# Padding zeros written on chip, 64-row query loads, and a planner order shifted by a table of moves

## Chip, cores and metric

One Trainium2 chip, one core. The metric is the device time of one execution in microseconds (us). The kernel before takes 840.61 us, the median of 3 runs (840.38 to 841.45).

## What is computed

Block-causal attention over 4 batches of 8 heads (576 positions, 64 dimensions), then two feed-forward layers on the 2304 tokens. The reference, cut to what matters:

```python
scores = scale * np.matmul(q, k.transpose(0, 1, 3, 2))
mask = block_i >= block_j                      # blocks of 64 positions
scores = np.where(mask, scores, -1000000000.0)
scores = scores - np.max(scores, axis=-1, keepdims=True)
attn = np.exp(scores)
attn = attn / (np.sum(attn, axis=-1, keepdims=True) + 1e-09)
attn_out = np.matmul(attn, v)                  # then to x, 2304 tokens by 512
h = np.maximum(np.maximum(x @ w1, x @ w2), x @ w3)      # 512 -> 768
x = h @ w_out                                           # 768 -> 512
h = np.maximum(x @ w_in, 0.0)                           # 512 -> 2048
return h * h @ w_out                                    # 2048 -> 512
```

## The kernel before, in words

The program has two parts. The **first part** (`fused_kernel` down to the first `nc.issue()`, line 862) holds all attention, the first feed-forward layer of four of the six token blocks (`mlp1(0)` to `mlp1(3)`) and the preparation of the weights. The **second part** holds `mlp1(4)`, `mlp1(5)` and the second feed-forward layer (`up`, `down`: tiles `ph_x`, `ph_z`, `acc_x`, `acc_z`, `acc_y`).

Attention goes by pairs of heads: 16 pairs, 4 per batch. A pair's `step(i)` makes, for 128 queries and two heads, the scores (`sc` in PSUM), writes the mask value into a corner and takes the row maximum on VectorE (`nm`), takes the exponential on ScalarE (`P`, with the row sums `sm`), transposes `P` on TensorE (`tp`) and copies the result back to SBUF (`ta`, `tb`); `values` multiplies with V (`av`). A pair has 25 transposes. The first four pairs (batch 0) are split in two groups of queries: group 0 (256 queries, steps 0 and 1) of all four pairs runs first, so that block 0 of the feed-forward layer can start.

Scores of two heads that share a tile are kept apart by zeros: head 0's queries stand in partitions 0 to 63 of one tile (`z[0]`), head 1's in partitions 64 to 127 of another (`z[1]`), and the other 64 partitions of each are zero. In `score_operands_f32` (line 499) these zeros come with the transfer: the input array `z0` holds them, and a 128x256 transfer (128 KB) brings each half of group 0. The tiles are `zk` (pairs 0 and 1) and `zk_early` (pairs 2 and 3), with the keys in the third slot.

The first feed-forward layer (`mlp1_`, tiles `l`, `run`, `hh`, `hl`, `ys`) is TensorE's filler: 288 matmuls for each block, whose blocks are 256, 320, 432, 432, 432 and 432 tokens wide. Its weights come as raw 64-bit numbers (`raw_w`, `raw_wo`, 512 KB each, 24 chunks) and are turned into a high and a low part (`w1h`, `w1l`, `wo`) by a chain for each chunk: two ScalarE passes, two VectorE passes, one GpSimd addition, one ScalarE cast, one VectorE subtraction (`load_w_`, line 398).

The order is set by a planner (`Plan`). The code only notes operations; `issue` (line 229) then plays them with fixed costs, picks at each step the engine that could start first, and on it the operation of lowest rank, then lowest number:

```python
t = min(start.values())
i = min((i for i, s in start.items() if s <= t), key=lambda i: (ops[i].rank, i))
```

Each engine runs its instructions in the order in which they were issued. All transfers go through SyncE's one queue; the built program keeps eight of their semaphores in turn, so that a transfer is issued only when the one eight before it has landed.

Of the kernel before, what the change touches and what calls it, by code (L numbers as in the profile page):

```python
# [12 lines left out]
F32 = mybir.dt.float32  # L13
# [10 lines left out]
B, H, S, D = 4, 8, 576, 64  # L24
# [13 lines left out]
TAIL = 512  # L38

GROUPS = ((0, 256), (256, 320))  # L40
GA, GB = 256, 320
# [6 lines left out]
CFG = dict(PD=-1, PE=1, A1=0, A2=0, WP=1, FC=(8, 16), WO=24, FI=0, LO2=0, HI2=0, Q2=0, RN=3, XL=2, HL=2, SO=0, TF=0, W_A=0.7, W_B=1.5, SPARE='hl..rhl..rhl..r..r..r', S=15, PB=3, QB=(2, 2, 3), BANKS=(3, 2, 1, 2), LO=0, HI=0, Q=0, EV=('*', '*'), EV2=('a', 'a'), CB=2, PC=0, PM=1000, PX=-0.5, PO=0, HH='*', XH='*', N0='a', YS='a', HIS=0, RB=1, TB=(1, 1), KB=1, CT='a', LT='d', XA=4, XB=0)  # L48
# [44 lines left out]
class View:  # L93


    def __init__(self, tile, area, steps=()):
        self.tile, self.area, self.steps = tile, area, steps
# [50 lines left out]
        return View(t, t.area)  # L148


class Op:
    def __init__(self, index, engines, name, args, kw, rank):
        self.index, self.engines, self.name, self.args, self.kw, self.rank = index, engines, name, args, kw, rank
        self.deps, self.after, self.makes = set(), [], []
        self.engine = self.end = None

# [15 lines left out]
class Plan:  # L172
# [53 lines left out]
            (v.tile.writes if any(v is x for x in out) else v.tile.reads).append((op, v.area))  # L226
        return op

    def issue(self):

        ops, free, held, queue = self.ops, self.free, self.held, self.queue
        left = [0 for op in ops]
        users = [[] for _ in ops]
        for op in ops:
            for d in (*op.deps, *op.after):
                if d.end is None:
                    left[op.index] += 1
                    users[d.index].append(op)
        waiting = {e: {} for e in free}
        narrow = False  # L240

        def offer(op):
            for e in op.engines:
                when = 0.0
                for d in op.deps:
                    when = max(when, d.end + ((SEM[d.engine] + (500 if e == 'pe' else 100 if e == 'pool' else 0)) if d.engine != e else 0))
                waiting[e][op.index] = when, shares_port(e, op)

        for op in ops:
            if not left[op.index]:  # L250
                offer(op)
        for _ in ops:
            best = None
            for e, w in waiting.items():
                if not w:
                    continue
                other = held["pool" if e == "dve" else "dve"] if e in held else 0.0
                start = {i: max(free[e], at, other if port else 0.0) for i, (at, port) in w.items()}
                t = min(start.values())
                i = min((i for i, s in start.items() if s <= t), key=lambda i: (ops[i].rank, i))  # L260
                if best is None or t < best[0]:
                    best = t, e, i
            t, e, i = best
            op = ops[i]
            op.engine = e
            length = duration(e, op) * SLOW[e]
            if e == "pe":
                length += SWITCH * (columns(op) != narrow)
                narrow = columns(op)
            if e in held and waiting[e][i][1]:  # L270
                held[e] = t + length - HOLD[e]
            for other in op.engines:
                del waiting[other][i]
            if e == "sp":
                queue = max(t + 1700, queue) + transfer(op)
                op.end, free[e] = queue + 300, t + 465
            else:
                op.end = t + length
                free[e] = op.end - LAP[e]
            for tile in op.makes:  # L280
                tile.make()
            self.tc.keep_in_program_order(self.call(self.real[e], alias(e, op.name), op.args, op.kw))
            for u in users[i]:
                left[u.index] -= 1
                if not left[u.index]:
                    offer(u)
        self.ops, self.queue = [], queue
# [15 lines left out]
def width(x):  # L303
    return math.prod(x.area.shape[1:])
# [5 lines left out]
def columns(op):  # L310
    return op.name != "transpose" and width(op.args[1] if op.args[1:] else op.kw["lhsT"]) <= 64


def alias(engine, name):
    return {"act": "copy", "dve": "tensor_copy"}.get(engine, name) if name in ("copy", "tensor_copy") else name


def shares_port(engine, op):
    if engine not in ("dve", "pool"):
        return False  # L320
    sources = [x for k, x in op.kw.items() if k.startswith("in") and isinstance(x, View) and not x.psum]
    if engine == "pool" or len(sources) > 1:
        return bool(sources)
    return bool(sources) and not op.kw["out"].psum and width(op.kw["out"]) % 2 == 0 and op.name != "tensor_reduce"


def duration(engine, op):
    views = op.views()
    n = max(map(width, views))
    psum = any(x.psum for x in views)  # L330
    if engine == "pe":
        if op.name == "transpose":
            return 109
        stat = op.args[1] if op.args[1:] else op.kw["lhsT"]
        n = width(op.args[0])
        if stat.tile.args[1] == F32:
            return n * (0.842 if width(stat) <= 64 else 1.69)
        return 1 + 0.4527 * n
    if engine == "act":
        if op.name == "activation":  # L340
            return 340 + 0.87 * n if "accum_out" in op.kw else 195 + 0.95 * n
        return 157 + 0.84 * n if psum else 190 + 0.85 * n
    if engine == "pool":
        return 160 + 2.26 * n
    if engine == "sp":
        return 430
    if op.name == "memset":
        return 58 + 0.84 * n
    if op.name == "reciprocal":
        return 160  # L350
    if op.name in ("tensor_scalar", "tensor_copy", "copy") and not psum:
        return (210 if isinstance(op.kw.get("scalar1"), View) else 155) + 0.52 * n
    return 150 + 1.046 * n


def transfer(op):
    x = next(v for v in op.views())
    return 35 + x.area.shape[0] * 4 * width(x) / 385.0
# [3 lines left out]
def fused_kernel(ctx: ExitStack, tc: tile.TileContext, z0, k0, kz0, qk, v, w123, wo1, win2, wo2, out):  # L362
    nc = Plan(tc)
# [19 lines left out]
    at = Pool(nc, es_a.enter_context(tc.tile_pool(name="at", bufs=1, side="right", reuse_waits="tile")))  # L383
# [115 lines left out]
    def score_operands_f32(n, g):  # L499


        if g == 0:
            if n < 2:
                zk = at.tile([128, 3, GA], F32, tag="tb", bufs=2 * CFG["TB"][1], name=f"zk{n}")
            else:
                if not early:
                    early.append(m1.tile([128, 8, 3, GA], F32, tag="wo1", name="zk_early"))
                zk = early[0][:, n]
            z, k = [zk[:, h] for h in range(2)], zk[:, 2]
            parts = (0, GA), (GA, GA)  # L510
        else:
            parts = (2 * GA, TAIL - GA + 128), (TAIL + GA + 128, TAIL - GA)
            z = [at.tile([128, w], F32, tag=t, bufs=CFG["QB"][2 * (t == "kl")], name=f"z{n}_{t}")
                 for t, (_, w) in zip(("qs", "kl"), parts)]
            k = at.tile([128, S], F32, tag="kh", bufs=CFG["QB"][1], name=f"k{n}")
        (o0, w0), (o1, w1) = parts
        nc.sync.dma_start(out=z[0], in_=z0[n, :, o0:o0 + w0])
        nc.sync.dma_start(out=k, in_=k0[n, :, :GROUPS[g][0] + GROUPS[g][1]])
        nc.sync.dma_start(out=z[1], in_=z0[n, :, o1:o1 + w1])
        return [[(z[h], k)] for h in range(2)], [(z[0][:, TAIL - GA:], k)] if g else None  # L520

    def value_operands(n, g):
        chunks = 2 if n < NPAIR and g == 0 else 5
# [4 lines left out]
    ops, x_t = {}, {}  # L528
# [16 lines left out]
    def prefetch(n, g):  # L545


        f32 = bool(n < NPAIR and g == 0 or S_F32[n])
        with nc.ranked(CFG["PO"]):
            ops[n] = f32, score_operands_f32(n, g) if f32 else score_operands(n), value_operands(n, g)  # L550
# [306 lines left out]
    with nc.behind(marks[CFG["WO"]][0]), nc.ranked(2):  # L857
        for q in range(NQ):
            quad_forms(1, q)
        for q in range(EARLY):  # L860
            quad_forms(0, q)
    nc.issue()
    es_a.close()


# [310 lines left out]
```

## Time and profile before

| | |
|---|---|
| median of 3 runs | 840.61 us |
| profiled execution, its own time | 840.18 us |
| its span, first to last instruction | 838.4 us |
| TensorE (PE) busy in the span | 825.8 us, 99% |
| VectorE (DVE) busy | 625.0 us, 75% |
| ScalarE (ACT) busy | 474.4 us, 57% |
| GpSimd (POOL) busy | 108.0 us, 13% |
| HBM read / written | 150.47 MB / 38.80 MB |

Shares over the whole span hide that the two parts differ: the first part ends near 364 us, and from there on TensorE runs one matmul after the other to the end. A busy TensorE is not one at its peak, since the ends of matmuls are modelled and overlap; what one matmul costs in a full stream is read from long unbroken pieces of the chain.

### The profile page before, as it was taken

The numbers are of one execution on the slowest core, as the hardware profiler recorded it, in microseconds if no ns is written. First come the engines' busy times: TensorE is split into PE (matmuls) and PEld (weight loads), VectorE is DVE, ScalarE is ACT, GpSimd is POOL, SyncE is SP. The second block draws the span as 40 slices with busy tenths as digits, with TensorE's granted clock in tenths as the row PEclk, the third lists the DMA queues.
The fourth block names the chain that finished last, engine by engine and source line by source line (L and its number), as shares of the span: only waits on it lengthen the run. The fifth ranks groups of instructions, "written<-read, shape, count | busy, mean of one in ns | idle before, by whom it ended". The sixth has DMA issues, their size and how long they took to land.

```text
span 838.4 us, 14621 instructions
## 1 busy us (share of the span) xinstructions
PE 825.8 (99%) x5008; PEld 779.2 (93%) x5008; DVE 625.0 (75%) x1347; ACT 474.4 (57%) x1099; POOL 108.0 (13%) x98
## 2 busy tenths in 40 slices
PE   8999999999999999999999999999999999999998
PEld 6678899988999889999999999999999999999998
DVE  7989789888889988817877557987269855478562
ACT  7999678788778767736554224544124552233441
POOL 2343111221122212202221000000000000000000
PEclk9999999999999999999999999999999999999999
DMA  9755455665566656254796867888988889988882
GB/s 326 263 162 171 124 175 182 203 224 183 167 206 206 199 192 201 77 194 150 264 352 228 312 203 248 286 292 271 306 257 255 257 249 288 293 256 254 246 272 85
DMA packets 92203, 190.24 MB, mean 227 GB/s; under 512 B 9697, under 2 KB 18913, under 8 KB 92129
## 3 DMA queue, kind: packets, MB, share of 16 engines
q1 hardware_dynamic: 92128, 189.31, 69.2%
q8 instruction: 40, 0.66, 0.3%
q14 instruction: 35, 0.28, 0.1%
HBM read 150.47 MB, written 38.80 MB: 226 GB/s over the span
## 4 chain that ended last, share of the span: by engine, by line
PE 90%; DVE 5%; ACT 3%; DMA 1%; POOL 1%; issue 1%; POOLq 0%; ACTq 0%; DVEq 0%
PE l L190 33%; PE ph_x L190 12%; PE acc_x L190 12%; PE ph_z L190 9%; PE acc_z L190 6%; PE av L190 4%; PE sc L190 4%; PE tp L190 3%; PE acc_y L190 3%; PE sc_t L190 2%; DVE nm L190 1%; DMA raw_w<-in_wo 1%; PE tp_t L190 1%; DVE w1l L190 1%; ACT P L190 1%
## 5 line engine op out<-in xcount | busy, mean ns | idle before, releaser
L190 PE MATMUL l<-xhl,w1h 128*128 128x432 f32 (+2 forms) x864 | 230.6, 344 | 0.5 <-DVE xhl L190 0.5
L190 PEld LDWEIGHTS l<-xhl,w1h 128*128 128x128 f32 x864 | 154.0, 188 | 7.5 <-DVE xhl L190 1.2
L190 PE MATMUL l<-xhl,w1l 128*128 128x432 f32 (+2 forms) x432 | 149.7, 347 | 0.6 <-DVE run L190 0.5
L190 PEld LDWEIGHTS l<-xhl,w1l 128*128 128x128 f32 x432 | 81.3, 188 | 5.8 <-DVE run L190 1.4
L190 PE MATMUL ph_x<-t,ws 128*128 128x384 f32 x432 | 80.9, 335 | 0.0
L190 PE MATMUL l<-hh,wo 128*128 128x432 f32 (+2 forms) x288 | 77.5, 344 | 1.2 <-DVE wo L190 1.1
L190 PEld LDWEIGHTS ph_x<-t,ws 128*128 128x128 f32 x432 | 75.6, 188 | 0.0
L190 ACT ACTIVATE P<-sc,nm 128x128 f32<-128x128 f32 (+3 forms) x128 | 67.3, 535 | 11.5 <-DVE nm L190 10.0
L190 DVE TENSOR_TENSOR run<-l,run 128x432 f32<-128x432 f32 (+2 forms) x72 | 39.8, 553 | 32.6 <-PE l L190 29.4
L190 POOL TENSOR_TENSOR f_w<-f_w,raw_w 128x512 int32<-128x512 int32 x30 | 41.5, 1384 | 148.2 <-DVE f_w L190 33.4
L190 DVE TENSOR_REDUCE nm<-sc 128x2 f32<-128x256 f32 (+2 forms) x96 | 55.0, 590 | 0.8
L190 PEld LDWEIGHTS l<-hh,wo 128*128 128x128 f32 x288 | 51.9, 188 | 3.7 <-DVE wo L190 1.3
L190 PE MATMUL acc_x<-g_p,ws 128*128 128x384 f32 x288 | 54.0, 335 | 0.0
L190 PE MATMUL ph_z<-b,ws 128*128 128x384 f32 x288 | 53.9, 335 | 0.0
L190 PE MATMUL tp<-ident,P 128*128 128x128 f32 x320 | 49.9, 275 | 1.1 <-ACT rs L190 0.5
L190 PEld LDWEIGHTS acc_x<-g_p,ws 128*128 128x128 f32 x288 | 50.5, 188 | 0.0
L190 PEld LDWEIGHTS ph_z<-b,ws 128*128 128x128 f32 x288 | 50.4, 188 | 0.0
L190 PE MATMUL l<-hl,wo 128*128 128x432 f32 (+2 forms) x144 | 49.2, 342 | 0.0
L190 PEld LDWEIGHTS tp<-ident,P 128*128 128x128 f32 x320 | 38.8, 141 | 8.9 <-ACT P L190 1.3
L190 PE MATMUL av<-tb,v 128*64 128x320 f32 (+1 forms) x256 | 42.9, 410 | 0.0
L190 ACT COPY tb<-tp 128x384 f32<-128x384 f32 (+1 forms) x64 | 32.4, 539 | 13.4 <-PE tp L190 12.9
L190 DVE TENSOR_TENSOR g_p<-c_wo,g_p 128x768 fp32r<-128x768 f32 x24 | 22.9, 956 | 16.8 <-ACT g_p L190 16.8
(188 smaller groups left out, 1746.5 us busy)
## 6 DMA issues: line engine op xcount, KB each, us to landing
ws<-ws_d SPq DMA_DIRECT2D x336, 256.0 KB, 4.0
ws_d<-wst SPq DMA_DIRECT2D x70, 256.0 KB, 4.4
raw<-in_qk SPq DMA_DIRECT2D x24, 576.0 KB, 4.3
ws_d<-wst SPq DMA_DIRECT2D x21, 512.0 KB, 7.1
raw_w<-in_w SPq DMA_DIRECT2D x18, 512.0 KB, 4.8
raw_w<-in_wo SPq DMA_DIRECT2D x16, 512.0 KB, 4.3
raw_wi<-in_win SPq DMA_DIRECT2D x14, 512.0 KB, 5.8
v<-in_v SPq DMA_DIRECT2D x16, 320.0 KB, 3.8
```

Of the source, the lines that this page charges most:

```text
L190: return getattr(engine, op_name)(*map(value, args), **{k: value(x) for k, x in kw.items()})
```

## The change

In group 0 of pairs 0 to 3, GpSimd writes the zeros (two memsets of 64x256 for each pair, rank -2), and the transfers bring the 64 filled partitions alone. The other case of `score_operands_f32` is written out again without a difference. `issue` takes a table of moves: for some 430 operations of the first part it adds a number to the rank and another to the place that decides between equal ranks. The planner also gets a cost for a GpSimd memset.

```diff
+MOVES = (
+    (8, -18, 7349), (18, -21.5, -8878), (19, -16.5, -4442), (20, -16, -3840), (21, -15.5, 1495), (43, -12.5,
...
+)
...
+        self.place = rank, index
...
-    def issue(self):
+    def issue(self, moves=()):
...
+        for i, rank, place in moves:
+            ops[i].place = ops[i].rank + rank, ops[i].index + place
...
-                i = min((i for i, s in start.items() if s <= t), key=lambda i: (ops[i].rank, i))
+                i = min((i for i, s in start.items() if s <= t), key=lambda i: ops[i].place)
...
+    if engine == "pool" and op.name == "memset":
+        return 100 + 0.8 * n
...
-            parts = (0, GA), (GA, GA)
...
+            with nc.ranked(-2):
+                nc.gpsimd.memset(z[0][64:128], 0.0)
+                nc.gpsimd.memset(z[1][0:64], 0.0)
+            nc.sync.dma_start(out=z[0][0:64], in_=z0[n, 0:64, 0:GA])
+            nc.sync.dma_start(out=k, in_=k0[n, :, :GA])
+            nc.sync.dma_start(out=z[1][64:128], in_=z0[n, 64:128, GA:2 * GA])
+            return [[(z[h], k)] for h in range(2)], None
...
-    nc.issue()
+    nc.issue(MOVES)
```

The same instructions are issued as before, and eight memsets; three copies that either ScalarE or VectorE may do go to VectorE instead of ScalarE. The order changes on every engine. Three places:

**SyncE, the first transfers.** `raw_w_0_0`, `raw_w_0_1` and `raw_w_0_2` are the first weight chunks, `zk` the queries (from `in_z`) and keys (from `in_k`) of pairs 0 and 1, `zk_early` those of pair 2, `v` the values. Before:

```order
L190 DMA raw_w_0_0_80<-in_w 128x1024
L190 DMA zk_82<-in_z 128x256
L190 DMA zk_82<-in_k 128x256
L190 DMA zk_82<-in_z 128x256
L190 DMA v_0_93<-in_v 128x256
L190 DMA raw_w_0_1_97<-in_w 128x1024
L190 DMA zk_99<-in_z 128x256
L190 DMA zk_99<-in_k 128x256
L190 DMA zk_99<-in_z 128x256
L190 DMA v_0_103<-in_v 128x256
L190 DMA raw_w_0_2_105<-in_w 128x1024
L190 DMA zk_early<-in_z 128x256
```

Now:

```order
L256 DMA raw_w_0_0_80<-in_w 128x1024
L256 DMA v_0_82<-in_v 128x256
L256 DMA zk_84<-in_z 64x256
L256 DMA zk_84<-in_k 128x256
L256 DMA zk_84<-in_z 64x256
L256 DMA raw_w_0_1_106<-in_w 128x1024
L256 DMA zk_91<-in_z 64x256 x2
L256 DMA zk_91<-in_k 128x256
L256 DMA v_0_112<-in_v 128x256
L256 DMA raw_w_0_2_114<-in_w 128x1024
L256 DMA zk_early<-in_z 64x256
L256 DMA zk_early<-in_k 128x256
```

The values of pair 0 moved ahead of its queries, and the five query loads here carry 64 partitions instead of 128.

**ScalarE, from the first weight chunk to the first exponentials** (`P_0_0`, `P_1_0`: steps 0 and 1 of pair 0). Before:

```order
L190 ACTIVATE raw_w_0_0_80<-raw_w_0_0_80 128x512 x2
L190 ACTIVATE raw_w_0_1_97<-raw_w_0_1_97 128x512
L190 CAST w1h_136<-raw_w_0_0_80 128x512
L190 ACTIVATE P_0_0_145,sm_0_146<-sc_0_0_117,nm_0_128 128x128 x2
L190 ACTIVATE P_1_0_158,sm_0_146<-sc_1_0_119,nm_1_133 128x256 x2
```

Now:

```order
L256 ACTIVATE raw_w_0_0_80<-raw_w_0_0_80 128x512 x2
L256 ACTIVATE raw_w_0_1_106<-raw_w_0_1_106 128x512 x2
L256 CAST w1h_149<-raw_w_0_0_80 128x512
L256 ACTIVATE P_0_0_160,sm_0_161<-sc_0_0_125,nm_0_134 128x128 x2
L256 ACTIVATE P_1_0_171,sm_0_161<-sc_1_0_129,nm_1_140 128x256 x2
```

The second pass over chunk `raw_w_0_1` moved ahead of the first exponentials.

**TensorE, the first scores and transposes** (pairs 0, 1 and 2). Before:

```order
L190 MATMUL sc_0_0_117<-zk_82 128x128
L190 MATMUL sc_1_0_119<-zk_82 128x256
L190 MATMUL sc_0_0_117<-zk_82 128x128
L190 MATMUL sc_1_0_119<-zk_82 128x256
L190 MATMUL sc_0_0_149<-zk_99 128x128
```

Now:

```order
L256 MATMUL sc_0_0_125<-zk_84 128x128 x2
L256 MATMUL sc_1_0_129<-zk_84 128x256 x2
L256 MATMUL sc_0_0_151<-zk_91 128x128 x2
L256 MATMUL sc_1_0_158<-zk_91 128x256 x2
L256 MATMUL tp_0_0_173<-ident,P_0_0_160 128x128 x2
```

Both heads of step 0 now stand before step 1, where the heads were taken one after the other.

## Rows read from the trace of the kernel before

**Rows 1.** The page's section 1, whole execution.

```profile
PE 825.8 (99%) x5008; PEld 779.2 (93%) x5008; DVE 625.0 (75%) x1347; ACT 474.4 (57%) x1099; POOL 108.0 (13%) x98
```

**Rows 2.** Windows: busy us and count of PE, PEld, DVE, ACT, POOL; clock; DMA.

```profile
0.00:100.00 100.00, 92.30 (x668) 73.08 (x669) 84.54 (x216) 84.93 (x217) 34.24 (x30) 1.00 0.63 211
100.00:364.00 264.00, 262.74 (x1710) 240.59 (x1709) 227.63 (x652) 201.09 (x565) 54.51 (x54) 1.00 0.57 184
...
372.00:485.00 113.00, 113.00 (x580) 108.45 (x579) 79.47 (x140) 53.96 (x99) 19.27 (x14) 1.00 0.70 248
...
10.00:20.00 10.00, 8.99 (x67) 6.04 (x66) 9.95 (x31) 9.59 (x32) 3.87 (x3) 1.00 1.02 369
```

**Rows 3.** Chain of waits in order of time: start us, us, what.

```profile
46.52 3.94 PE l L190 x33
...
157.33 1.31 PE l L190 x9
...
304.11 0.48 PE sc_t L190 x2
...
308.20 0.17 PE sc L190 x2
308.81 0.24 PE sc L190 x2
309.44 0.35 PE sc L190 x2
310.56 0.87 PE tp L190 x8
...
321.69 0.93 PE sc L190 x4
...
338.35 3.01 PE av L190 x23
...
364.29 120.32 PE l L190 x614
...
826.46 8.35 PE acc_x L190 x48
```

**Rows 4.** Groups of PE by form, to 364.2 us: xcount | busy us, mean ns | idle.

```profile
L190 PE MATMUL r<-ident,sm 128*64 128x128 f32 x64 | 5.0, 277 | 0.9 <-DVE nm L190 0.6 <-DVE sm L190 0.2
```

**Rows 5.** Waits of PE, longest first: us in total, times, longest us.

```profile
PE sc L190 <- DMA zk<-in_k: 1.4, 1, 1.4
...
PE l L190 <- DVE wo L190: 1.1, 1, 1.1
...
PE sc_t L190 <- ACT P L190: 0.5, 1, 0.5
```

**Rows 6.** Timeline, first 14 us: start us, us, engine, instruction, [idle before <-releaser].

```profile
0.73 0.20 POOL masks.py:197 MEMSET ident<- 128x128 f32 x1 [0.29 <-POOLq L1169]
...
1.36 3.78 PE L190 MATMUL idle<-ident 128*128 128x128 f32 x16 [1.36 <-POOL ident masks.py:199]
...
4.40 1.24 ACT L190 ACTIVATE raw_w<-raw_w 128x512 f32<-128x512 f32 x2 [2.18 <-DMA raw_w<-in_w]
5.10 0.43 DVE L190 TENSOR_SCALAR raw_w<-raw_w 128x512 int32<-128x512 int32 x1 [4.24 <-ACT raw_w L190]
...
5.27 2.04 PE L190 MATMUL sc<-zk 128*128 128x128 f32 x8
...
6.40 1.28 POOL L190 TENSOR_TENSOR raw_w<-raw_w 128x512 int32<-128x512 int32 x1 [5.09 <-DVE raw_w L190]
...
6.98 0.17 DVE L190 MEMSET sc<- 64x128 f32 x1 [0.72 <-PE sc L190]
...
7.88 0.66 ACT L190 ACTIVATE raw_w<-raw_w 128x512 f32<-128x512 f32 x1 [2.24 <-DMA raw_w<-in_w]
...
8.74 1.55 PE L190 MATMUL sc<-zk 128*128 128x128 f32 x8 [1.42 <-DMA zk<-in_k]
...
8.95 0.36 ACT L190 ACTIVATE P<-sc,nm 128x128 f32<-128x128 f32 x1
```

More of the change, by code (lines that the diff above doesn't have):

```diff
@@ L509, in score_operands_f32 @@
             z, k = [zk[:, h] for h in range(2)], zk[:, 2]
-            parts = (0, GA), (GA, GA)
[L511 to L515, printed above, removed]
+            with nc.ranked(-2):
[5 more added lines that the diff above has]
+            return [[(z[h], k)] for h in range(2)], None
+        parts = (2 * GA, TAIL - GA + 128), (TAIL + GA + 128, TAIL - GA)
+        z = [at.tile([128, w], F32, tag=t, bufs=CFG["QB"][2 * (t == "kl")], name=f"z{n}_{t}")
+             for t, (_, w) in zip(("qs", "kl"), parts)]
+        k = at.tile([128, S], F32, tag="kh", bufs=CFG["QB"][1], name=f"k{n}")
         (o0, w0), (o1, w1) = parts
         nc.sync.dma_start(out=z[0], in_=z0[n, :, o0:o0 + w0])
-        nc.sync.dma_start(out=k, in_=k0[n, :, :GROUPS[g][0] + GROUPS[g][1]])
+        nc.sync.dma_start(out=k, in_=k0[n])
         nc.sync.dma_start(out=z[1], in_=z0[n, :, o1:o1 + w1])
-        return [[(z[h], k)] for h in range(2)], [(z[0][:, TAIL - GA:], k)] if g else None
+        return [[(z[h], k)] for h in range(2)], [(z[0][:, TAIL - GA:], k)]
     def value_operands(n, g):
```

60 rows, old and new, of the table MOVES are left out of this document.

## The prediction

> **What bounds the kernel now.** I read the page's busy shares first, then the windows, then the chain, the waits of TensorE and the start of the timeline. TensorE is busy for 825.8 of 838.4 us [rows 1], so whatever the change gives must come out of TensorE's own stream. The chain shows where that stream has holes and where it has none: from 364.29 us it is one piece of 614 feed-forward matmuls in 120.32 us, 196 ns each, and it goes on without a break to the last piece, which starts at 826.46 and lasts 8.35 [rows 3]. That is 834.8; the 3.6 us behind it are the last copies and the last transfer. The change leaves all of this as it is, so the end moves by as much as 364.29 moves. Vector work in the second part leaves room: 79.47 of 113 us are busy at 372 to 485 us [rows 2], so an earlier TensorE does not run into weights that are not ready.
>
> **What the first part could take at best.** The full-stream price of each kind of matmul is read from unbroken pieces of the chain [rows 3], the counts from the loops. Feed-forward: 288 of 256 columns at 119 ns (3.94 us for 33) make 34.4 us; 288 of 320 columns at 146 ns (1.31 for 9) make 41.9; of the 576 of 432 columns 38 are in the long piece at the end (614 less the 576 of blocks 4 and 5), and the other 538 at 196 ns make 105.4. Transposes: 16 pairs x 25 at 109 ns (0.87 for 8) make 43.5. Values: 16 x 3.01 make 48.2. Scores of the last twelve pairs: 24 heads x (0.17 + 0.24 + 0.35 + half of 0.93) make 29.4. The pieces of 288 columns: 32 x 0.48 make 15.4. Scores of the first four pairs at that rate of 1.67 ns a column: 8 heads x 1280 columns make 17.1. Together 335.3 us. TensorE's first score starts at 5.27 [rows 6], and 364.29 - 5.27 = 359.0. So 23.7 us are not explained by full-stream work. Up to some 6 of them are the row sums, of which the larger form has 5.0 us of busy time [rows 4] and which both orders have; the other 18 are waits, seen and unseen, and changes of shape. This 18 is the most that any order can win.
>
> The windows tell where: in the first 100 us ScalarE is busy 84.93 us of the 95.6 since its first pass at 4.40, VectorE 84.54 of the 94.9 since 5.10 [rows 2, 6]. They have lost 10.7 and 10.4 us, and TensorE, which feeds them and is fed by them, about as much. From 100 to 364 us ScalarE has 63 us to spare and VectorE 36, and TensorE shows only 264 - 262.74 = 1.26 us of idle time [rows 2]. In the first 100 us it shows 100 - 92.30 = 7.70; less the 1.36 before its first matmul and 0.13 between warm-up and first score, that is 6.2, and 1.42 of these are one wait for a transfer [rows 6], which leaves 4.8 of waits for the vector engines, such as 1.1 for a weight chunk [rows 5].
>
> **The change, part by part.** *Memsets.* Eight memsets of 256 columns on GpSimd. The only row near is the 128-column one of 0.20 us [rows 6]: at double that, 0.4 each, eight take 3.2 us behind TensorE's warm-up start at 1.36, so to about 4.6, before GpSimd's first addition at 6.40, which waits for VectorE anyway [rows 6]. Between nothing and 0.4 each, I take nothing; without that cover the first additions would come up to 3.2 us late. The first two end near 2.2 and are not what the first score waits for.
>
> *Transfers.* At 10 to 20 us the queue is full: share 1.02 at 369 GB/s [rows 2], that is 0.36 us for 128 KB. The second pair's scores waited 1.42 us for their keys, to 8.74 [rows 6]. Counting down to those keys, 1792 KB stood in the queue (two weight chunks, three query loads, two key loads, one of values) and now stand 1664 (the same with four half query loads). That is 128 KB less, so **0.36 us earlier**. The second weight chunk, for which ScalarE waited 2.24 us to 7.88 [rows 6], also has 128 KB less ahead of it. The first pair now has the values ahead, 64 KB more in sum, 0.18 us later; in return step 0 of both heads comes first, and VectorE, which waited 0.72 us to 6.98 for the third score product [rows 6], needs only two. I set these two against each other. No 64-partition transfer is in the trace. If such a transfer took as long as a 128-partition one, the bytes would count as 1920 KB, and the keys would come 0.36 us later. So the ends are -0.36 and +0.36; I take -0.36, since the full queue's rows go by bytes.
>
> A page of the Trainium skill speaks against this: SBUF — State Buffer, section Door 1: the DMA port swizzle, says that a transfer into partitions 0 to 63 reaches half of the ports and measured 196 GB/s for it against 328 for all 128. By that the saved bytes would save no time, and the sum would be that of the +0.36 end.
>
> *Order, first 100 us.* All engines keep their work; the table only changes who waits for whom. The ends are 0 and -10.4, VectorE's whole loss (a loss instead of a gain is a rival below). The nearest rows are TensorE's own visible waits of 4.8 us: these are single waits of 0.5 to 1.1 us that a filler matmul put ahead of the waiting one can cover, and the filler is there. Not all, since at the start no filler exists: its first weights pass through chains that begin at 4.40. I take three quarters, **-3.5 us**.
>
> *Order, 100 to 364 us.* The ends are 0 and about -7 (18 less the 10.7). Visible are 1.26 us, such as one wait of 0.5 before `sc_t` [rows 5]. I take **-1.0**.
>
> *A wait that is added.* ScalarE now makes both passes over the second weight chunk ahead of the first exponentials. After the chunk lands these are two passes and a cast of about 0.64 each, so the exponentials start near 7.88 - 0.36 + 1.92 = 9.4 instead of 8.95 [rows 6], 0.5 later; behind them wait the first transposes. The same pass is then missing later on the same engine, which is nearly full, so I count nothing, and make it a rival.
>
> **Sum.** -0.36 - 3.5 - 1.0 = -4.9 on the profiled execution's 840.2 gives 835.3. The median of the runs shown is 840.61, 0.4 above that execution, so 835.7.
>
> **Rivals.** *(a) The half transfers take as long as whole ones.* Same order gains, but +0.36 in place of -0.36: 836.4. For it: nothing in the rows excludes it. Against it: in a full queue a neighbour may fill what one leaves free. 0.17.
>
> *(b) Waits only change places.* In the first 100 us three engines have nearly equal work, so TensorE freed at one place waits at the next for the same exponential; then only the transfers count: 840.61 - 0.36 = 840.2. For it: ScalarE's and VectorE's 85 of 95 us, and that every operation is still there. Against it: 10 us of loss on each is much for engines with so many independent chunks. 0.14.
>
> *(c) Slower, by conversions that stand ahead of exponentials.* The place is ScalarE's queue in the first 100 us, as above: an exponential 0.5 us later holds the transposes of its pair, and with them the copies and the next scores. If five of the eight half-pairs of that stretch pay 0.5 and nothing is won: +2.5, so 843.1. It decides once the new waits outnumber the old: some ten of 0.5 eat the 4.9. For it: the planner plays fixed costs, and a table that fits these closely leaves less slack for real ones. Against it: TensorE's fillers cover 0.5 easily once block 0 runs. 0.14.
>
> *(d) The order fits much better.* All visible waits (4.8 + 1.26 + 0.36) and 4 of the unseen: -10.4, 830.2. It would need ScalarE nearly gapless. 0.05.
>
> **The numbers.** The forecast has 0.50. What a measurement of this kernel can tell from no change is 0.2%, 1.7 us. Forecast, (a) and (d) are faster: 0.72; (b) is no change: 0.14; (c) is slower: 0.14. The range goes from (d), 830.5, to 841.5, which takes in (b) and the milder half of (c).
>
> **What would show it.** On GpSimd eight memsets before 5 us. The second pair's scores near 8.4 instead of 8.74; a start at 9 or later speaks for (a). In the window to 100 us TensorE's idle time near 4 instead of 7.7 and more matmuls than 668 [rows 2]. The long piece of feed-forward matmuls starts near 359.5 instead of 364.29. The forecast is wrong if that start stays or moves back: with new waits of TensorE for `P` in the first 100 us it is (c), with the same total under other names (b).

## The result and the profile after

The changed kernel takes **844.16 us** (median of 6 runs, 843.62 to 844.95), the kernel before on the same chip 839.87 (6 runs, 838.57 to 841.45). The ratio is 1.0051, 95% interval 1.0038 to 1.0065: slower by 4.3 us, where 4.9 us less were forecast. It lies outside the range.

The page's section 1 of the profiled execution after (844.42 us, span 842.6), against [rows 1]:

```profile
PE 830.7 (99%) x5008; PEld 783.4 (93%) x5008; DVE 625.5 (74%) x1350; ACT 473.7 (56%) x1096; POOL 108.7 (13%) x106
```

TensorE is busy for 4.9 us more with the same 5008 matmuls, and the span is 4.2 longer. The loss is not idle time, so it should be longer or less overlapped matmuls. The windows after, in the columns of [rows 2]:

```profile
0.00:100.00 100.00, 92.91 (x646) 74.18 (x646) 86.17 (x215) 84.16 (x215) 35.71 (x38) 1.00 0.63 203
100.00:364.00 264.00, 263.72 (x1697) 241.10 (x1697) 225.38 (x654) 198.32 (x556) 53.69 (x54) 1.00 0.55 181
```

To 100 us TensorE has started 22 matmuls fewer than before (646 against 668), to 364 us another 13. Its visible idle time fell in both windows, from 7.70 to 7.09 and from 1.26 to 0.28, and still it is behind. So what was lost should be in the matmuls' own time, and the chain of waits shows where (start us, us, what; the first two rows are the values of pair 3):

```profile
93.16 2.14 PE av L256 x11
95.96 1.41 PE av L256 x7
...
115.44 3.01 PE av L256 x23
...
159.67 3.55 PE av L256 x23
...
229.26 2.86 PE av L256 x25
...
248.34 3.50 PE av L256 x26
268.92 4.52 PE av L256 x26
...
375.32 113.11 PE l L256 x578
488.43 2.08 PE ph_x L256 x12
...
829.78 8.35 PE acc_x L256 x48
```

and of before a group of the same size and form, twenty records of pair 1:

```profile
57.15 2.21 PE av L190 x20
```

A matmul of `values` leaves two records in the trace. Before, the matmuls of a later pair (14, so 28 records, of which the chain lists 22 or 23) took 3.01 us each time, as in [rows 3]. After, pair 4 still takes 3.01, but pair 6 3.55, pair 10 3.50 and pair 11 4.52, and pair 3's twenty take 2.14 + 1.41 instead of 2.21. Together 0.54 + 0.49 + 1.51 + 1.34 = 3.9 us. Pair 9 goes the other way, 2.86, 0.15 less. The long piece of feed-forward matmuls starts at 375.32 instead of 364.29, with 578 matmuls instead of 614, so that its start says little; its end does. The second part moves along: its first `ph_x` starts at 488.43 instead of 484.61, the last piece of 8.35 at 829.78 instead of 826.46 [rows 3].

What the groups have in common is read from the order. For each piece of a head's V there is one matmul for head 0 and one for head 1; the two are called a couple here. `values` writes head 0 to PSUM partitions 0 to 63 and head 1 to 64 to 127, in matmuls of 64 stationary columns. Before, the heads alternate, `tb_0` with `tb_1`, all but one couple, whose first matmul stands ahead of the four of `av_0`. The table gives each matmul a number of its own, and in pair 11 the couples are apart:

```
L256 MATMUL av_1_3759<-tb_0_3643,v_0_3246 64x320
L256 MATMUL av_0_3763<-ta_3537,v_0_3246 64x256
L256 MATMUL av_0_3763<-ta_3537,v_0_3246 64x128
L256 MATMUL av_0_3763<-ta_3537,v_0_3246 64x256
L256 MATMUL av_0_3763<-ta_3537,v_0_3246 64x128
L256 MATMUL av_1_3759<-tb_0_3643,v_0_3246 64x320 x2
L256 MATMUL av_1_3759<-tb_0_3643,v_0_3246 64x192
L256 MATMUL av_1_3759<-t_11_3733,v_0_3246 64x64
L256 MATMUL av_1_3759<-tb_1_3651,v_0_3246 64x320 x3
L256 MATMUL av_1_3759<-tb_1_3651,v_0_3246 64x192
L256 MATMUL av_1_3759<-t_11_3733,v_0_3246 64x64
```

The planner cannot see a cost in this. `duration` gives every matmul of 64 stationary columns 0.842 ns a column, half of the 1.69 for wider ones, wherever it stands.

The start of the timeline after, in the columns of [rows 6]:

```profile
2.81 1.39 POOL L256 MEMSET zk_early<- 64x256 f32 x4
...
5.78 3.02 PE L256 MATMUL sc<-zk 128*128 128x128 f32 x8 [0.62 <-DMA zk<-in_k]
...
8.73 1.22 ACT L256 ACTIVATE raw_w<-raw_w 128x512 f32<-128x512 f32 x2 [3.00 <-DMA raw_w<-in_w]
...
9.54 2.90 PE L256 MATMUL sc<-zk 128*128 128x128 f32 x8 [0.75 <-DMA zk<-in_k]
...
10.35 0.36 ACT L256 ACTIVATE P<-sc,nm 128x128 f32<-128x128 f32 x1
```

The last memset ends at 4.2. The second weight chunk, the second pair's keys and the first exponential are all later than before: 8.73 against 7.88, 9.54 against 8.74, 10.35 against 8.95 [rows 6]; these are single executions. The DMA share and the GB/s (last two columns) of three windows of 1 us, after:

```profile
5.00:6.00 1.00, 0.38 (x2) 0.25 (x2) 0.77 (x2) 0.73 (x2) 0.00 (x0) 1.00 0.91 225
...
7.00:8.00 1.00, 1.00 (x4) 0.82 (x4) 0.59 (x2) 0.00 (x0) 0.87 (x1) 1.00 1.02 250
8.00:9.00 1.00, 0.80 (x2) 0.07 (x1) 0.11 (x1) 0.27 (x1) 0.00 (x0) 1.00 0.99 230
```

and before:

```profile
5.00:6.00 1.00, 0.87 (x4) 0.76 (x4) 0.87 (x2) 0.64 (x2) 0.00 (x0) 1.00 1.01 366
...
7.00:8.00 1.00, 0.32 (x2) 0.00 (x0) 0.91 (x4) 0.12 (x1) 0.68 (x1) 1.00 1.06 359
8.00:9.00 1.00, 0.26 (x2) 0.29 (x3) 1.00 (x4) 1.00 (x3) 0.00 (x0) 1.00 1.08 399
```

The engines of the queue are about as busy, and bring 30 to 42% less. In the window between these, 6 to 7 us, the change brings 344 against 370.

### The profile page after: what moved, and what is told of

The parts are those of the page before. It is cut to its first block, busy times and chain, and to the rows that moved or that the text cites. A ratio compares the mean times of both kernels' runs of the same rounds, so it can differ in the third digit from the quotient of the medians.

```text
span 842.6 us, 14596 instructions
## 1 busy us (share of the span) xinstructions
PE 830.7 (99%) x5008; PEld 783.4 (93%) x5008; DVE 625.5 (74%) x1350; ACT 473.7 (56%) x1096; POOL 108.7 (13%) x106
## 4 chain that ended last, share of the span: by engine, by line
PE 91%; DVE 6%; ACT 1%; issue 1%; DMA 1%; SPq 0%; DVEq 0%; ACTq 0%
PE l L256 34%; PE acc_x L256 12%; PE ph_x L256 12%; PE ph_z L256 9%; PE acc_z L256 6%; PE av L256 5%; PE sc L256 4%; PE tp L256 4%; PE acc_y L256 3%; PE sc_t L256 2%; DVE nm L256 1%; DVE w1l L256 1%; DVE f_w L256 1%; PE tp_t L256 1%; DMA zk<-in_k 1%
## 5 line engine op out<-in xcount | busy, mean ns | idle before, releaser
L256 ACT ACTIVATE P<-sc,nm 128x256 f32<-128x256 f32 (+3 forms) x128 | 67.1, 532 | 15.3 <-DVE nm L256 11.4
L256 DVE TENSOR_REDUCE nm<-sc 128x1 f32<-128x384 f32 (+2 forms) x96 | 54.2, 587 | 0.8
L256 PE MATMUL av<-tb,v 128*64 128x320 f32 (+1 forms) x256 | 46.1, 410 | 0.0
L256 PEld LDWEIGHTS av<-tb,v 128*64 128x64 f32 x256 | 26.2, 137 | 11.4 <-ACT t L256 1.7
```

Source lines behind the costliest of these rows:

```text
L256: return getattr(engine, op_name)(*map(value, args), **{k: value(x) for k, x in kw.items()})
```

## Experiments

Three theories. **P**: the couples that the table pulled apart. **L**: the 64-row loads bring the first operands later. **C**: TensorE's first scores run at half the pace (3.02 and then 2.90 us for eight, where before needed 2.04 and then 1.55). Every kernel here replays a written-out order instead of the planner's loop. "Table's order" is that of the change. Each was timed beside the kernel before on the same chip, and a ratio is always to it. That kernel stands at 839.84 for the runs with heads one after the other, alternating throughout and the table's order alone, at 839.73 for the change with its couples together and the three splices, and at 839.56 for the others. The ratio with its 95% interval does not always agree with the quotient of the two medians (0.9982 for the table's order alone, where 839.13 / 839.84 is 0.9992), so a difference of less than about 1 us between two of these kernels is not settled.

### Couples side by side again, six groups

```diff
 table's order, pair 11 (so too the values of pairs 3, 6, 10 and the row sums of pair 0)
-av_1<-tb_0 64x320, ..., av_1<-tb_0 64x320 x2, ..., av_1<-tb_1 64x320 x3
+av_1<-tb_0 64x320, av_1<-tb_1 64x320, av_1<-tb_0 64x320, av_1<-tb_1 64x320, ...
```

> The changed kernel's order on every engine, but in five value groups (av3_1, av6_1, av10_1, av11_0, av11_1) and one row-sum group (r0_0) TensorE's matmuls of the two heads alternate again, as they do before. Theory P (a head's 64-column matmul overlaps the other head's when they alternate, and the table pulled them apart): the profile of the change shows these groups at 3.55 instead of 3.01 (av6), 3.50 (av10), 4.52 (av11) and 2.14 + 1.41 instead of 2.21 (av3), together 3.9 us above the unbroken ones, so 844.2 - 3.9 = 840.3, from 839.8 to 841. Rival theory L (the loss is made at the start, by the half loads): no more than 0.5 us off, 843.7 to 844.2, since the freed time is waited away elsewhere.

840.49 us, ratio 1.0007 (0.9999 to 1.0016): 3.7 us less than the change, by the place of nineteen couples. The chain at pairs 6, 10 and 11:

```profile
158.42 3.01 PE av L403 x23
...
246.57 2.96 PE av L403 x26
266.58 2.85 PE av L403 x28
```

3.55, 3.50 and 4.52 became 3.01, 2.96 and 2.85. P holds; L asked for 843.7 or more.

### Heads one after the other in the kernel before

```diff
 order of before, second groups of pairs 8 to 11
-head 0, head 1, head 0, head 1, ...
+all five of head 0, all five of head 1
```

> The kernel before, its order on every engine, but in four value groups (av8_1 to av11_1) all of head 0's five matmuls stand ahead of all of head 1's. Theory P: each such group costs 1.5 to 2.05 us more (1216 columns at 1.684 ns once more, 2.05; the one group that the table split in full showed 4.52 instead of 3.01), so 6 to 8 us more: 845.6 to 847.6. Rival: other work covers it, at most 2 us more.

846.17 us, ratio 1.0072 (1.0057 to 1.0086): +6.3 us for four groups. All four stand in the chain like the first:

```profile
202.65 4.52 PE av L401 x26
...
278.19 4.52 PE av L401 x26
```

Four times 4.52 - 3.01 make 6.0 of the 6.3. It is the same 4.52 as pair 11's in the change, which also has all five couples of its second group apart. Nothing but TensorE's order differs from the kernel before here, so the price belongs to the order alone.

### Alternating throughout in the kernel before

```diff
 order of before, pairs 4 to 15
-av_1<-tb_0 64x320, av_0 (four), av_1<-tb_1 64x320, ...
+av_0 (four), av_1<-tb_0 64x320, av_1<-tb_1 64x320, ...
```

> The kernel before, its order on every engine, but in twelve value groups (pairs 4 to 15) the first matmul of head 0, which stands five places ahead of its partner, is moved next to it, so that the heads alternate all through. Theory P: a group's 1600 columns at 1.684 ns, both heads at once, are 2.69 us where the trace shows 3.01, so 0.32 each and 12 x 0.32 = 3.8 us less: 836 from 839.6, and groups of about 2.7 to 2.8 in the chain. Rival: two lone matmuls of the same half at the ends of a group overlap with their neighbours already, or the freed time is waited away: 839.2 to 839.8.

838.29 us, ratio 0.9984 (0.9974 to 0.9995): 1.5 us less. The direction is right, the size under half. All twelve groups read like these:

```profile
182.00 2.85 PE av L401 x28
...
224.60 2.85 PE av L401 x28
```

12 x (3.01 - 2.85) = 1.9. I had charged the matmul that stands ahead a full price of its own; the chain shows that it cost only 0.16 a group.

### The table's order with whole loads

```diff
-nc.gpsimd.memset(z[0][64:128], 0.0)
-nc.gpsimd.memset(z[1][0:64], 0.0)
-nc.sync.dma_start(out=z[0][0:64], in_=z0[n, 0:64, 0:GA])
+nc.sync.dma_start(out=z[0], in_=z0[n, :, 0:GA])
```

and so for `z[1]`.

> The changed kernel's order on every engine, with the loads of before (128 partitions, zeros from memory) and no memsets. Theory L (the 64-partition loads are slower than whole ones: the second weight chunk landed for ScalarE at 8.73 instead of 7.88, and the first scores run at 2.90 us per eight instead of 1.55 until 14 us): the keys come earlier by 0.3 to 0.8 us, the first eight scores of the second pair take 1.55 again, and the time falls by 1 to 2, to 842.2 to 843.2. Theory P alone: nothing, 844.0 to 844.4.

843.98 us, ratio 1.0049 (1.0036 to 1.0062): 0.2 from the change, nothing that can be told. A miss for L.

### The order of before with 64-row loads

```diff
+nc.gpsimd.memset(z[0][64:128], 0.0)
+nc.gpsimd.memset(z[1][0:64], 0.0)
-nc.sync.dma_start(out=z[0], in_=z0[n, :, 0:GA])
+nc.sync.dma_start(out=z[0][0:64], in_=z0[n, 0:64, 0:GA])
```

with the eight memsets first on GpSimd, the order of before otherwise.

> The order of before on every engine, with the 64-partition loads and the eight memsets put ahead of GpSimd's other work. Theory L: the mirror of the run before, slower by 1 to 2 us, 840.9 to 841.9 against 839.9. By bytes alone (my forecast): 0.36 faster, 839.5. If the half loads cost nothing either way: 839.9.

840.56 us, ratio 1.0012 (1.0002 to 1.0022): +1.0 us, and the interval leaves out the 0.36 us less of the byte count. In the order of before the 64-row loads cost something; in the table's order, above, no cost could be told.

### Two more warm-up matmuls

```diff
-    for _ in range(8):
+    for _ in range(10):
         mm(idle
```

> The changed kernel with ten warm-up matmuls instead of eight, so that TensorE has no hole of 0.62 us ahead of its first score. Theory C (that hole alone keeps the first scores at the lower clock level, 1.2 GHz, until 14 us): the second pair's eight scores take 1.55 instead of 2.90 us, and the time falls by 0.5 to 1.5, to 842.7 to 843.7. If ScalarE and VectorE set the pace of the start anyway: faster scores but 844.0 to 844.3.

844.08 us, ratio 1.0053 (1.0041 to 1.0065). The timeline of its profiled execution:

```profile
6.05 1.55 PE L403 MATMUL sc<-zk 128*128 128x128 f32 x8
...
9.44 1.55 PE L403 MATMUL sc<-zk 128*128 128x128 f32 x8 [1.84 <-DMA zk<-in_k]
```

Eight scores in 1.55 us instead of 3.02 and 2.90, and the kernel takes as long. The saved time went into a longer wait for the keys (1.84 instead of 0.75). So the slow start is worth nothing that can be told. That the two matmuls made it fast is not shown: the change with its couples together, below, has eight warm-up matmuls and a longer hole (1.24 us instead of 0.62), and its profiled execution runs the first eight scores in 1.68 us and the next in 1.55.

### The table's order alone

```diff
 whole loads, as above; table's order
+all 29 couples that stood apart: head 0 and head 1 side by side
```

> The table's order with the loads of before, no memsets, and all 29 separated couples of the heads' matmuls rejoined. Theory P, with the table worth nothing else: the same as the alternating kernel before, near 836 if that holds, near 839.6 if that gains nothing. If the table's order is worth something once its couples are whole: 1 us or more below that kernel. Rival theory that the table's order also has longer waits elsewhere: 1 us or more above it.

839.13 us, ratio 0.9982 (0.9971 to 0.9993). Beside the order of before with its couples together (0.9984, 0.9974 to 0.9995) the table makes no difference that can be told; by the medians it is 0.8 us slower.

### The change with its couples together

```diff
 open loads of 64 rows, memsets, table's order, as in the change
+all 29 couples that stood apart: head 0 and head 1 side by side
```

> The change as it is (64-row loads, memsets, the table's order), with all 29 couples side by side; against e6_table_alternate_whole the loads alone differ. In the order of before the loads cost 1.0 us, in the table's order with its couples apart nothing (844.16 against 843.98). If they cost what they cost in the order of before: 839.1 + 1.0 = 840.1 us. If the table covers them: 839.1.

838.62 us, ratio 0.9991 (0.9982 to 1.0000). Its second pair's scores start at 9.54 and its first exponential at 10.28, as late as in the change. Beside the same order with whole loads (839.13, ratio 0.9982) no cost of the loads shows; by the ratios up to 0.8 us of it could still be there.

### Where the table loses and wins

Matched matmul by matmul, the trace of the table's order (whole loads, couples together) falls 3.5 us behind that of the alternating kernel in the first 68 us of TensorE's work and gets back some 2 by 196. Is the one a loss and the other a gain of its own? Three splices, with whole loads and all couples together:

```diff
+late:   order[:780 of before] + the rest as the table has it
+early:  order[:792 of the table] + the rest as before has it
+middle: late, and from 196 us of TensorE's work on again as before has it
```

> Whole loads, all couples side by side. Up to some 79 us the order of before (as in e5_alternate), from there the order of the table (as in e6_table_alternate_whole). Matched matmul by matmul, the record of e6 is 3.5 us behind that of e5 after 68 us of TensorE's work, 1.2 behind after 196 us and 1.6 at the end. Theory T (the table's early order loses some 3 us for good, its middle wins some 2 on its own): 838.3 - 1.9 = 836.4 us. Rival V (what the early part loses the middle only gets back, since the vector engines have then a head start; an order that does not lose has nothing to get back): 838.3, within 0.8 of e5.

837.68 us, ratio 0.9978 (0.9968 to 0.9988).

> The other way round: up to some 79 us the order of the table, from there that of before, whole loads, all couples side by side. Theory T: the early loss of 3.5 us stays, 838.3 + 3.2 = 841.5 us. Rival V: most of it is got back later, 838.5 to 839.5.

839.68 us, ratio 0.9999 (0.9990 to 1.0008).

> As e8_late_table, but from 196 us of TensorE's work on again the order of before. Theory T: the table loses another 0.4 us there, so 836.0 us, 0.4 under e8. Rival V: 838.3, as e8.

838.16 us, ratio 0.9981 (0.9973 to 0.9990).

Late and middle agree with V: where nothing was lost early, the table's middle wins no 1.9 us, only 0.6 against 838.29, inside the intervals. Early lies between: 1.4 us of the 3.2 that T asked for. By this, more than half of what an early order loses would come back by itself. It is not shown: the 3.2 comes from one execution of each of two kernels (837.92 and 840.33, where their medians are 838.29 and 839.13), and 1.4 is near what can be told at all. The spliced "late" kernel beats before and after and is the fastest of all runs, though not by more than its interval against the alternating kernel.

## Why the prediction was wrong, by its own steps

The miss is 844.16 - 835.7 = 8.5 us: 4.9 that were to be won and were not, and 4.3 that were lost, less the 0.7 by which the kernel before's median fell from 840.61 to 839.87 with more runs. The loss and the missing gain have different causes.

**The step that failed is the price of the stream.** The floor of the first part counted "Values: 16 x 3.01" and took every kind of matmul at one price whatever stands beside it; so the order's terms could only be waits, with ends "0 and -10.4" and "0 and about -7". But 3.01 was the price of couples in alternation, all but one. It was no floor either: with that couple put together the group takes 2.85. By the runs, couples apart cost the change 844.16 - 838.62 = 5.5 us (5.0 by the ratios), and those that before itself has apart cost it 839.84 - 838.29 = 1.5 (1.3). What the table and the 64-row loads do besides, 838.62 - 838.29 = 0.3, is not told from nothing. That 5.5 - 1.5 + 0.3 gives the measured 4.3 proves nothing, since the two kernels between cancel in this sum. The rows are the check: 3.9 - 0.15 from the groups above and 12 x 0.16 = 1.9 for the one couple a group that already before has apart make 5.65, against 5.5.

A page of the Trainium skill bears on this: TensorEngine Tiling (Array Packing), section Key Properties, says that tiles of a tiled array work independently and can run matmuls in parallel, and its section Available Configurations lists two tiles for 64 columns. The trace agrees as far as the couples alternate. Of a pair whose heads stand one after the other only the second group is so ordered, and the first takes 0.70 us in that kernel and in the alternating one (by the timelines, from 202.58 to 203.28 and from 181.93 to 182.63). So 3.82 us stand against 2.15, a factor of 1.78.

**Order, first 100 us: -3.5 forecast, nothing found.** This is the missing gain, and the second step that failed: that a wait which is covered early is won at the end. Idle time near 4 and more than 668 matmuls were asked for; 7.09 and 646 came. With the couples together the two orders stand at 100 us like this, that of before first:

```profile
0.00:100.00 100.00, 93.07 (x666) 74.16 (x667) 82.82 (x216) 84.67 (x216) 34.56 (x30) 0.98 0.63 211
```

```profile
0.00:100.00 100.00, 91.62 (x651) 73.54 (x652) 86.78 (x216) 84.74 (x216) 33.03 (x30) 0.97 0.63 208
```

The table is 15 matmuls behind, and its kernel is no slower by the ratios (0.9982 against 0.9984), 0.8 us by the medians. What was read as winnable (waits of 0.5 to 1.1 us) did go, the wait for `wo` among it, and other waits came. TensorE's waits after, up to 365 us, in the columns of [rows 5]:

```profile
PE av L256 <- DMA v<-in_v: 1.2, 1, 1.2
PE l L256 <- ACT run L256: 0.8, 1, 0.8
PE l L256 <- DVE run L256: 0.8, 2, 0.4
PE l L256 <- ACT P L256: 0.7, 1, 0.7
```

Nearest to this is rival (b), waits that change places, which had 0.14, though the visible idle time did fall by 1.6 us in the first 364. The splices suggest why that gave nothing: a position lost early may come back in part, so that a wait of the first 100 us would not be worth its length at the end. **Order, 100 to 364 us: -1.0 forecast.** The visible idle time fell by 0.98, as asked, and the split groups of pairs 4 to 11, 0.54 + 0.49 + 1.51, took more.

**Transfers: -0.36 forecast, between 0 and +1.0 found.** The second pair's scores started at 9.54, later than 8.74 and past the end of +0.36, and by the prediction's own mark this speaks for (a). But the mark was a poor one, since that start varies from execution to execution. With whole loads and the start of before it is 8.49 in the kernel with heads one after the other, and in the alternating one

```profile
9.78 2.63 PE L401 MATMUL sc<-zk 128*128 128x128 f32 x8 [2.34 <-DMA zk<-in_k]
```

What speaks against counting bytes is the rate: at about the same share the windows show 225 to 250 GB/s instead of 359 to 399. In the order of before the loads cost 1.0 us, in the table's nothing that could be told: 844.16 against 843.98, 838.62 against 839.13.

The rule of the Trainium skill that the prediction weighed (SBUF — State Buffer, Door 1: the DMA port swizzle) agrees with the trace in direction: loads of half the partitions come at a lower rate. Its two figures put the rate at 0.6 of the full one; the windows, which mix these loads with whole ones, show 0.58 to 0.70. By the same figures, as an estimate, half a load would take 0.84 of a whole load's time, so that the prediction's "no time" saved was a little too strict.

**Memsets: right.** Eight, the last ended at 4.2 (4.6 forecast), and GpSimd's first addition waits for VectorE as before.

**The added wait on ScalarE: 0.5 forecast, 1.4 came, worth nothing that can be told.** Part of the 1.4 may be scatter: the alternating kernel, with ScalarE's order of before, has its first exponential at 9.99. The change with its couples together has it at 10.28 and takes 838.62 us. So rival (c) forecast the right side and nearly the right time, 843.1, by a mechanism that is not the one.

**The second part: right.** Its start and its end moved by 3.3 to 3.8 us with the end of the first, though the wrong way.

## What to carry to other kernels

Matmuls of 64 stationary columns that fill two halves of the array are priced in couples: keep the two next to each other, and let no search over single instructions or planner see half the price without its partner (here 1.5 us on a group of 3). Before a full-stream price from a chain goes into a floor, look at what stands beside the matmul in the order, and whether the change alters that. A transfer to half of the partitions is not half a transfer: ask the windows for its rate. A wait near the start of a long program need not be worth at the end what it lasts; here a start that ran its first scores at half the pace cost nothing that could be told.

## What was unexpected of the hardware

The two halves give only what alternation gives: 28 records in 2.85 us when strictly alternating, 3.01 us where one matmul of head 0 stands five places ahead of its partner, 4.52 where the second group has all of head 0 ahead of head 1. In pair 9 of the change one matmul stands ahead too, but the second couple of `av_0` has head 1 first, and the pair takes 2.86; why is not tested.

The first scores can run at half the pace without a price. In the kernel that alternates in the order of before, TensorE does little from 8 to 10 us, while it waits for keys, and then the granted clock (third column from the end) falls to 0.52, about the lower of the two levels (1.2 of 2.4 GHz):

```profile
8.00:10.00 2.00, 0.22 (x2) 0.25 (x3) 1.22 (x4) 1.08 (x3) 0.00 (x0) 1.00 1.04 393
10.00:12.00 2.00, 2.00 (x8) 1.72 (x8) 1.50 (x4) 2.00 (x10) 0.00 (x0) 0.52 1.05 319
```

That execution took 837.92 us. In the change eight scores also take twice the 1.55 us of the warmed kernel, but the column reads 1.00 there:

```profile
10.00:12.00 2.00, 2.00 (x8) 1.73 (x8) 1.68 (x5) 2.00 (x10) 0.95 (x1) 1.00 0.94 267
```

So the row does not confirm the lower level; only the pace of the matmuls suggests it. Nor does the hole ahead of the first score decide the pace: after 0.62 us it was half in the change, after 1.24 us nearly full in the change with its couples together (eight scores in 1.68 us).
